# The first indirect gather of the routed experts placed ahead of a unit's values, and at most five loads of q, k, v asked for at a time

## The chip, the core and the metric

The kernel runs on one core of a Trainium2 chip. The core has a matrix engine (TensorE, in the profile PE for the matmuls and PEld for the loading of weights), a vector engine (VectorE, DVE), an activation engine (ScalarE, ACT), a general engine (GpSimd, POOL) and a queue that only issues transfers (SyncE, SP). Sixteen DMA engines move the data. The metric is the device time of one execution in microseconds, as the median of several runs. One execution is profiled, and its trace tells of every instruction when it started, how long it took and what it waited for.

## What is computed

An attention block without softmax is followed by a mixture of experts with an early exit. Cut to what matters:

```python
# q, k, v: (8, 8, 576, 64) float32; g_norm: (64,)
kv  = einsum('bhsd,bhse->bhde', k, v)          # one 64x64 state per batch and head
o   = einsum('bhsd,bhde->bhse', q, kv)
rms = sqrt(mean(o * o, axis=-1) + 1e-6)
x   = (o / rms * g_norm)                       # to (4608 tokens, 512)

out = x.copy()
xc  = x[x @ w_skip > 0]                        # the tokens that are computed
logits = xc @ w_gate                           # 8 experts
e_idx  = argmax(logits, axis=1)
gate_w = softmax(logits)[e_idx]
for e in range(8):                             # w1[e]: 512x1024, w2[e]: 1024x512
    h = relu(xc[e_idx == e] @ w1[e])
    y[e_idx == e] = gate_w * (h @ w2[e])
out[x @ w_skip > 0] = xc + y
```

The tokens of an expert are known only once the logits are: the kernel numbers them, writes x to the output in memory, and fetches the rows of each expert from there by an indirect gather.

## The kernel before

**The attention part** goes through 36 units, numbered n = 0 to 35 (`NU`, line 433). A unit is a pair of 128-token tiles for half of the heads. Two units (u = 0 and 1) make up a pair of tiles, two pairs a batch, and after each four batches two more units take the ninth row of each group of nine tokens. The loop of lines 1035 to 1075 writes out the order of all engines by hand: what is emitted earlier stands earlier in the queue of its engine, and each engine works through its queue in order. In step n stand, one after the other: `turn(n + 1)`, the transposes of q for the next unit; `root(n - 1)`, the square root on ACT; the jobs put down for "early"; `values(n)`, the eight matmuls of q with the state into a PSUM tile and the square of the result on ACT; the jobs for "mid"; `squares(n)`, the reduce of these squares on DVE (line 531); the jobs for "squared"; `norm(n - 1)`, on DVE the reciprocal (line 545) and the multiplication (line 554, tile `xl`) for the unit before; the jobs for "pe", the small additions of `finish`; and at the end the jobs for "dve" and "end". Up to step 29 `squares(n)` stands behind `norm(n - 1)`; from step 30 (`THIRD + 2`, with `THIRD` = 28) it stands ahead of it and of the "squared" jobs.

`scale` (line 641) runs what `weigh` has put aside, the multiplication by g_norm on POOL (line 628). Called from `norm` it lets the POOL instruction wait for the reciprocal of that norm, and it puts down the store of a finished pair of tiles for a later step.

**Buffers.** The PSUM tiles of `values` come from a pool of two (`o_ps`), but units 30 and 33 (`THIRDS`) use the tile of the states, `sum_ps`, which is free by then. A unit's PSUM tile is free again when its norm has read it.

**The states** of batch b are summed up by `state` (line 387), in portions over several steps ahead of the batch's units, and stored in `kvd`.

**Loads.** `load_part` (line 116) issues one load of 288 KB on the SP queue. A batch has four of each of q, k and v: 96 loads in all. The first 32 (k, v of batch 0, q of 0, k, v of 1, q of 1, k, v of 2) are issued ahead of the loop. The buffers hold three batches of k and v and two of q; later loads wait for the buffer that a batch before has used. The stores of x and the loads of the experts' weights go through the same queue, which issues in order.

**The routing.** Tokens are numbered in three groups, after units 12, 22 and 36 (`ends`). The stream `gating(1)`, of the second group, gives out four pieces of DVE work at the end of each step; it ends with `early()` (line 913), which fetches the first 192 tokens of the first expert (`FIRST`, 128 and 64) among the tokens of the first 22 tiles, so that their first layer can start before the attention part ends. `early` makes two small tables on DVE (`ohc1`, `bv1`, lines 916 and 921), and then gives `put` to "mid" of step 30:

- `scale(30)`, 22 matmuls on the PE (line 941) that place row numbers into PSUM, and `turn(32)`, which the loop leaves out later;
- in "squared" of step 30, `put_rows`: the sum of two pieces of a row number on DVE (line 949), two index operations on DVE and the first gather, 128 rows, on POOL (lines 930, 932, 934); a matmul that moves the row numbers of the other 64 tokens (line 953); again two index operations and the second gather, a row being fetched in two halves.

`first_in` (steps 33 and 34, "pe") transposes the gathered rows (line 865), `first_layer_1` multiplies them with the first expert's w1 (line 876). The load of its w2 is issued in step 32, behind the last matmul of `values(32)`. `hits` (line 759) makes on DVE, in two halves of eleven tiles each, a table that is used after the attention part; the halves stand in "mid" of steps 31 and 33.

**Behind the attention part** the last group is chosen on DVE (lines 682 to 702), ranked on the PE (lines 713 to 719), numbered, and the experts follow, ordered by their number of tokens, on the PE with matmuls of lines 1180 to 1279.

Of the kernel before, what the change touches and what calls it, by code (L numbers as in the profile page):

```python
# [8 lines left out]
FP32 = mybir.dt.float32  # L9
BF16 = mybir.dt.bfloat16  # L10
I32 = mybir.dt.int32
AX = mybir.AxisListType
# [5 lines left out]
def kernel(  # L18
# [92 lines left out]
    g_ps = ps_g.tile([P, 512], FP32)  # L111
    GB = 4 * KD + 8 * G

    kts, vts, qts = {}, {}, {}

    def load_part(t, src, b, j):

        js = slice(j, j + 1)
        nc.sync.dma_start(
            out=t[:, js, :, :].rearrange("p j c d -> p j (c d)"),  # L120
            in_=src[b].rearrange("(j a) (p c) d -> (a p) j (c d)", a=2, c=C)[:, js, :])

    def load(pool, tag, src, b):
        t = pool.tile([P, 4, C, D], FP32, tag=tag, name=tag)
# [321 lines left out]

    late = []
    todo = {}
    WAIT = mybir.DependencyInfo(mybir.DependencyClass.Sync, mybir.DependencyReason.SCHED_ONLY)

    def at(step, part, job):
        todo.setdefault((step, part), []).append(job)
# [188 lines left out]
    def scale(n, behind=None, keep=0, eng=None):  # L641

        while len(late) > keep:
            job, nq, store = late.pop(0)
            ins = job(eng or nc.gpsimd)
            if behind:
                tc.add_manual_dep(ins.ins, behind.ins.name, WAIT, reason="VectorE's port is free then")
            store = store() if store else None
            if store:
                at(max(min(n + 2, NU + 1), store_from.get(nq, 0)), "end", store)  # L650
# [262 lines left out]
    def early():  # L913

        ohc = gat_pool.tile([P, NE, 2], BF16, tag="ohc1", name="ohc1")
        nc.vector.tensor_tensor(out=ohc[:, :, :], in0=hi_k[:, 0:NE].unsqueeze(2).to_broadcast([P, NE, 2]),
                                in1=colid_i[:, 0:2].unsqueeze(1).to_broadcast([P, NE, 2]),
                                op=ALU.is_equal)
        yield
        bv = gat_pool.tile([P, NE, 2, 2], BF16, tag="bv1", name="bv1")  # L920
        nc.vector.tensor_tensor(out=bv[:, :, :, :], in0=ohc[:, :, :].unsqueeze(3).to_broadcast([P, NE, 2, 2]),
                                in1=row_k[:, 0:NE, :].unsqueeze(2).to_broadcast([P, NE, 2, 2]),
                                op=ALU.mult)
        ps = g_ps[:, GB:GB + 4]

        def gather(ps, m, off):
            n = P // m
            src = keep.tile([P, 1], I32, name=f"src{m}")
            row = gat_pool.tile([P, 1], FP32, tag="row1", name="row1")
            nc.vector.tensor_scalar(out=row[:, :], in0=ps, scalar1=float(n), op0=ALU.mult,  # L930
                                    scalar2=part_of[m][:, 0:1], op1=ALU.add)
            nc.vector.scalar_tensor_tensor(out=src[:, :], in0=row[:, :], scalar=float(N * n),
                                           in1=row[:, :], op0=ALU.is_lt, op1=ALU.mult)
            nc.gpsimd.indirect_dma_start(
                out=x_of(xg0, off, m), out_offset=None, in_=cut_rows(m, KNOWN)[:, :],
                in_offset=bass.IndirectOffsetOnAxis(ap=src[:, 0:1], axis=0))

        def put():
            scale(now[0])
            for t in range(NE):  # L940
                nc.tensor.matmul(out=ps, lhsT=oha_k[:, t, :],
                                 rhs=bv[:, t, :, :].rearrange("p c i -> p (c i)"), start=(t == 0),
                                 stop=(t == NE - 1), skip_group_check=True)
            turn(now[0] + 2)
            turned_ahead.append(now[0] + 2)

            def put_rows():
                rows = gat_pool.tile([P, 2], FP32, tag="rows1", name="rows1")
                nc.vector.tensor_reduce(out=rows[:, :], in_=ps.rearrange("p (c i) -> p c i", i=2),
                                        axis=AX.X, op=ALU.add)  # L950
                gather(rows[:, 0:1], P, 0)
                more = g_ps[:, GB + 4:GB + 5]
                nc.tensor.matmul(out=more, lhsT=again[0, 64][:, :], rhs=rows[:, 1:2], start=True,
                                 stop=True, skip_group_check=True)
                gather(more, 64, P)
            assert now[0] == THIRD + 2
            at(now[0], "squared", put_rows)
        yield
        yield
        yield "mid", put  # L960

    load_kv(1)
    load_q(1)
# [62 lines left out]
    for part in range(2):  # L1026
        at(NU - 3 + part, "pe", lambda part=part: first_in(part))
    at(NU - 1, "early", lambda: first_layer_1(range(1), slice(0, P)))
    for part in range(2):
        at(NU - 5 + 2 * part, "mid", lambda part=part: known_at.append(  # L1030
            hits(part * NE // 2, NE // 2, colid_i, gat_pool, NE, known_at)))
    at(NU - 1, "end", first_rest)

# [1 line left out]
    for n in range(NU + 2):  # L1035
# [6 lines left out]
        if n < NU:  # L1042
            values(n)
        jobs(n, "mid")
        if THIRD + 2 <= n < NU:
            squares(n)
        jobs(n, "squared")
        done = norm(n - 1) if 1 <= n <= NU else None
        if n < THIRD + 2:
            squares(n)  # L1050
        jobs(n, "pe")
        if done:
            done()
# [601 lines left out]
```

## Time and profile before

| what | value |
|---|---|
| median of 3 runs | 369.1 us (367.73, 369.1, 369.5) |
| the profiled execution | 368.61 us, of which 366.7 us from the first to the last instruction |
| granted clock of the PE | 0.997 |
| busy: PE, DVE, ACT, POOL | 349.8, 247.6, 147.0, 123.2 us |
| moved by the DMA engines | 81.70 MB, 32808 packets, mean 223 GB/s |
| loads of q, k, v | 96 of 288 KB |
| the first indirect gather issued on POOL | 101.17 us |

The span goes from the first to the last instruction; the rest of the execution's time lies around it. Busy time is the time in which an engine had an instruction at work; a wait of an engine is put down to what ended last before it went on. Instructions that only issue a transfer are not busy time, and the time to landing runs from the issue to the signal that all of the transfer has arrived.

### The profile page before, as it was taken

What the parts mean: (1) busy time and instruction counts of PE and PEld (TensorE: products, weight loads), DVE (VectorE), ACT (ScalarE), POOL (GpSimd) and SP (SyncE); (2) the same over time, 40 slices, a digit from 0 to 9 for tenths busy, and PEclk for the clock granted to TensorE, in tenths of its full rate; (3) what the DMA queues carried; (4) which work ended last, traced back from release to release, by engine and by line L of the source; (5) the groups of instructions that cost most, each with busy time, mean ns of one, the idle gap of its engine ahead of it and who ended that gap; (6) DMA issues with size and microseconds to landing.
All of it is one profiled execution on the core that took longest, in us unless ns stands there. A gap on an engine that the chain in (4) does not pass through costs nothing.

```text
span 366.7 us, 9560 instructions
## 1 busy us (share of the span) xinstructions
PE 349.8 (95%) x3754; PEld 304.6 (83%) x3754; DVE 247.6 (68%) x630; ACT 147.0 (40%) x424; POOL 123.2 (34%) x201
## 2 busy tenths in 40 slices
PE   8979998999899998999999999999999999999993
PEld 4768887889779667599879988989988998989982
DVE  2646678678889553875937676686776776878821
ACT  2537675677855323345104402511431430531410
POOL 8037677757784170223032102303203203002002
PEclk9999999999999999999999999999999999999998
DMA  7999999999969479782526437365563662601001
GB/s 258 378 389 389 391 384 389 394 351 305 348 214 362 121 255 374 285 261 77 220 85 231 145 142 240 126 231 155 193 230 102 231 247 73 221 1 57 3 2 53
DMA packets 32808, 81.70 MB, mean 223 GB/s; under 512 B 3242, under 2 KB 3250, under 8 KB 32756
## 3 DMA queue, kind: packets, MB, share of 16 engines
q1 hardware_dynamic: 29264, 70.53, 54.2%
q0 software_dynamic: 3472, 10.48, 8.8%
q8 instruction: 31, 0.51, 0.5%
q14 instruction: 21, 0.17, 0.1%
q10 hardware_dynamic: 20, 0.02, 0.0%
HBM read 66.80 MB, written 14.48 MB: 222 GB/s over the span
## 4 chain that ended last, share of the span: by engine, by line
PE 79%; issue 7%; DMA 4%; DVE 3%; POOL 2%; ACT 2%; SPq 0%; POOLq 0%; DVEq 0%; ACTq 0%
PE bank L1279 45%; PE bank L1211 9%; PE o_ps L507 6%; DMA v<-in_v_dram 4%; PE sum_ps L387 4%; PE bank L1199 4%; PE q_ps L469 3%; PE bank L1180 2%; DVE xl L554 1%; DVE rs L531 1%; PE o_ps L488 1%; PE q_ps L876 1%; PE g_ps L876 1%; POOL xb L628 1%; PE g_ps L417 1%
## 5 line engine op out<-in xcount | busy, mean ns | idle before, releaser
L1289 ACT COPY p<-bank 128x128 f32<-128x128 f32 (+6 forms) x70 | 20.8, 297 | 96.8 <-PE bank L1279 89.3
L1279 PE MATMUL bank<-xt,w 128*128 128x128 f32 (+5 forms) x336 | 55.4, 288 | 0.4 <-DVE bank L1283 0.4
L1410 POOL DMA_INDIRECT out_dram<-xg,rows x14 | 14.0, 997 | 116.5 <-DVE xg L1407 114.2
L1279 PEld LDWEIGHTS bank<-xt,w 128*128 128x128 f32 x336 | 47.0, 190 | 2.3 <-DVE bank L1283 1.8
L1283 DVE TENSOR_TENSOR bank<-bank,p 128x128 f32<-128x128 f32 (+6 forms) x70 | 23.6, 337 | 30.0 <-PE bank L1279 27.6
L628 POOL TENSOR_TENSOR xb<-xl,g_b 128x512 f32<-128x512 f32 x26 | 31.7, 1221 | 15.0 <-DVE rs L545 12.1
L1279 PE MATMUL bank<-xs,s 128*128 128x128 f32 (+5 forms) x224 | 36.7, 289 | 0.0
L507 PE MATMUL o_ps<-kvd,qT 128*128 128x146 f32 x240 | 35.4, 289 | 0.7 <-DVE xl L554 0.5
L507 PEld LDWEIGHTS o_ps<-kvd,qT 128*128 128x128 f32 x240 | 31.4, 189 | 1.9 <-DVE xl L554 1.3
L1279 PEld LDWEIGHTS bank<-xs,s 128*128 128x128 f32 x224 | 31.1, 190 | 1.0 <-issue 0.5
L1211 PE MATMUL bank<-w,ht 128*32 128x128 f32 (+2 forms) x424 | 29.9, 313 | 0.0
L387 PE MATMUL sum_ps<-v,k 64*64 64x64 f32 x1152 | 24.5, 223 | 4.7 <-issue 4.3
L531 DVE TENSOR_REDUCE rs<-sq 128x8 f32<-128x512 f32 x36 | 24.5, 681 | 5.2 <-ACT sq L523 5.0
L387 PEld LDWEIGHTS sum_ps<-v,k 64*64 64x64 f32 x1152 | 20.2, 134 | 9.2 <-issue 6.1
L554 DVE TENSOR_TENSOR xl<-o_ps,rs 128x584 f32<-128x584 f32 x32 | 24.5, 766 | 3.9
L1211 PEld LDWEIGHTS bank<-w,ht 128*32 128x32 f32 (+2 forms) x424 | 18.2, 119 | 10.6 <-issue 7.2
L1279 PE MATMUL bank<-t,ht 128*128 128x256 f32 x112 | 27.0, 384 | 0.0
L1279 PE MATMUL bank<-w,ht 128*128 128x256 f32 x112 | 26.5, 380 | 0.0
L1171 POOL DMA_INDIRECT xg<-out_dram,src x14 | 13.9, 992 | 35.2 <-DMA out_dram<-xg,rows 19.0
L1279 PE MATMUL bank<-t,hs 128*128 128x256 f32 x112 | 25.3, 379 | 0.0
L523 ACT ACTIVATE sq<-o_ps 128x512 f32<-128x512 f32 x34 | 20.2, 595 | 11.3 <-PE o_ps L507 10.5
L1279 PEld LDWEIGHTS bank<-t,ht 128*128 128x128 f32 x112 | 20.8, 190 | 3.9 <-issue 1.2
(217 smaller groups left out, 671.9 us busy)
## 6 DMA issues: line engine op xcount, KB each, us to landing
w<-in_moe_w_dram SPq DMA_DIRECT2D x16, 2048.0 KB, 10.1
k<-in_k_dram SPq DMA_DIRECT2D x32, 288.0 KB, 6.0
v<-in_v_dram SPq DMA_DIRECT2D x32, 288.0 KB, 6.2
q<-in_q_dram SPq DMA_DIRECT2D x32, 288.0 KB, 6.0
out_dram<-xb SPq DMA_DIRECT2D x25, 256.0 KB, 5.9
out_dram<-w SPq DMA_DIRECT2D x8, 256.0 KB, 5.5
out_dram<-xb POOLq DMA_DIRECT2D x3, 256.0 KB
xg<-out_dram,src POOLq DMA_INDIRECT x16
```

What stands on the lines that cost most here:

```text
L387: nc.tensor.matmul(out=sum_ps[w * 64:(w + 1) * 64, a, u, :], lhsT=kt[r, 2 * u + w, c, :], rhs=vt[r, 2 * u + w, c, :], start=(c == 0), stop ...
L507: mm = nc.tensor.matmul(out=ps[:, w, 0:2 * PK].rearrange("p (r k) -> p r k", r=2)[:, :, cols], lhsT=qT[:, w, a, :], rhs=kvds[b % KVD][:, w ...
L523: nc.scalar.activation(out=sq[:, :, :, :], in_=heads(ps, G, G + 2 * D), func=ACT.Square)
L531: nc.vector.tensor_reduce(out=rs[:, :, :], in_=sq[:, :, :, :].rearrange("p x y (a d) -> p x (y a) d", a=2), axis=AX.X, op=ALU.add)
L554: nc.vector.tensor_tensor(out=xl[:, :, :, :].rearrange("p x y (a k) -> p x (y a) k", a=2), in0=ps[:, :, 0:2 * PK].rearrange("p x (h k) -> ...
L628: late.append((lambda eng: eng.tensor_tensor(out=xb[:, :, 4 * u * D:(4 * u + 4) * D].rearrange("p r (w x) -> p r w x", w=2), in0=xl[:, :, ...
L1199: nc.tensor.matmul(out=hps[:, cols], lhsT=w_sb[r][0][:, dc, f * P:(f + 1) * P], rhs=xt[:, dc, cols], start=(dc == 0), stop=(dc == DC - 1))
L1211: nc.tensor.matmul(out=yps[q * m:(q + 1) * m, 0:n], lhsT=ht(f)[:, off:off + m], rhs=w_sb[r][1][:, f, q * n:(q + 1) * n], start=(f == 0), s ...
L1279: nc.tensor.matmul(out=out, lhsT=lhsT(i), rhs=rhs(i), start=start and i == 0, stop=i == k - 1, skip_group_check=True)
L1283: nc.vector.tensor_tensor(out=to, in0=x, in1=y, op=ALU.add)
L1289: nc.scalar.copy(out=t, in_=x)
L1410: ins = nc.gpsimd.indirect_dma_start(out=cut_rows(m)[:, :], out_offset=bass.IndirectOffsetOnAxis(ap=rows[:, col:col + 1], axis=0), in_=x, ...
```

## The change

Two things are changed. First, `put` goes from "mid" to "early" of step 30: the 22 placing matmuls, the sum of the row number, the two index operations and the first gather stand ahead of `values(30)`. A second job, `again_more`, stands in "mid" of step 30: `turn(32)` and the matmul for the other 64 tokens. The second gather alone is left in "squared". `put` no longer calls `scale(30)`, so that the weighing of unit 28 is issued by `norm(29)`, behind the first gather and behind that norm's reciprocal. `squares(n)` stands ahead of `norm(n - 1)` only from step 32 on, and in steps 30 and 31 the "squared" jobs stand behind norm and squares. The second half of `hits` goes from step 33 to step 34.

Second, each load of q, k, v from the thirteenth on waits, on SP, for the landing of the fifth load before it. Stores and weights are not counted and not held by this themselves.

```diff
--- before.py
+++ after.py
@@ -111,14 +111,19 @@
     g_ps = ps_g.tile([P, 512], FP32)
     GB = 4 * KD + 8 * G
 
-    kts, vts, qts = {}, {}, {}
+    kts, vts, qts, loads = {}, {}, {}, []
+    PACED, DEPTH = 12, 5
+    WAIT = mybir.DependencyInfo(mybir.DependencyClass.Sync, mybir.DependencyReason.SCHED_ONLY)
 
     def load_part(t, src, b, j):
 
         js = slice(j, j + 1)
-        nc.sync.dma_start(
+        ins = nc.sync.dma_start(
             out=t[:, js, :, :].rearrange("p j c d -> p j (c d)"),
             in_=src[b].rearrange("(j a) (p c) d -> (a p) j (c d)", a=2, c=C)[:, js, :])
+        if len(loads) >= PACED:
+            tc.add_manual_dep(ins.ins, loads[-DEPTH].ins.name, WAIT, reason="a short queue")
+        loads.append(ins)
 
     def load(pool, tag, src, b):
         t = pool.tile([P, 4, C, D], FP32, tag=tag, name=tag)
@@ -446,7 +451,6 @@
 
     late = []
     todo = {}
-    WAIT = mybir.DependencyInfo(mybir.DependencyClass.Sync, mybir.DependencyReason.SCHED_ONLY)
 
     def at(step, part, job):
         todo.setdefault((step, part), []).append(job)
@@ -935,29 +939,29 @@
                 out=x_of(xg0, off, m), out_offset=None, in_=cut_rows(m, KNOWN)[:, :],
                 in_offset=bass.IndirectOffsetOnAxis(ap=src[:, 0:1], axis=0))
 
+        rows = gat_pool.tile([P, 2], FP32, tag="rows1", name="rows1")
+
         def put():
-            scale(now[0])
             for t in range(NE):
                 nc.tensor.matmul(out=ps, lhsT=oha_k[:, t, :],
                                  rhs=bv[:, t, :, :].rearrange("p c i -> p (c i)"), start=(t == 0),
                                  stop=(t == NE - 1), skip_group_check=True)
+            nc.vector.tensor_reduce(out=rows[:, :], in_=ps.rearrange("p (c i) -> p c i", i=2),
+                                    axis=AX.X, op=ALU.add)
+            gather(rows[:, 0:1], P, 0)
+            assert now[0] == THIRD + 2
+            at(now[0], "mid", again_more)
+
+        def again_more():
             turn(now[0] + 2)
             turned_ahead.append(now[0] + 2)
-
-            def put_rows():
-                rows = gat_pool.tile([P, 2], FP32, tag="rows1", name="rows1")
-                nc.vector.tensor_reduce(out=rows[:, :], in_=ps.rearrange("p (c i) -> p c i", i=2),
-                                        axis=AX.X, op=ALU.add)
-                gather(rows[:, 0:1], P, 0)
-                more = g_ps[:, GB + 4:GB + 5]
-                nc.tensor.matmul(out=more, lhsT=again[0, 64][:, :], rhs=rows[:, 1:2], start=True,
-                                 stop=True, skip_group_check=True)
-                gather(more, 64, P)
-            assert now[0] == THIRD + 2
-            at(now[0], "squared", put_rows)
-        yield
-        yield
-        yield "mid", put
+            more = g_ps[:, GB + 4:GB + 5]
+            nc.tensor.matmul(out=more, lhsT=again[0, 64][:, :], rhs=rows[:, 1:2], start=True,
+                             stop=True, skip_group_check=True)
+            at(now[0], "squared", lambda: gather(more, 64, P))
+        yield
+        yield
+        yield "early", put
 
     load_kv(1)
     load_q(1)
@@ -1026,8 +1030,8 @@
     for part in range(2):
         at(NU - 3 + part, "pe", lambda part=part: first_in(part))
     at(NU - 1, "early", lambda: first_layer_1(range(1), slice(0, P)))
-    for part in range(2):
-        at(NU - 5 + 2 * part, "mid", lambda part=part: known_at.append(
+    for part, (step, where) in enumerate(((NU - 5, "mid"), (NU - 2, "mid"))):
+        at(step, where, lambda part=part: known_at.append(
             hits(part * NE // 2, NE // 2, colid_i, gat_pool, NE, known_at)))
     at(NU - 1, "end", first_rest)
 
@@ -1042,12 +1046,12 @@
         if n < NU:
             values(n)
         jobs(n, "mid")
-        if THIRD + 2 <= n < NU:
+        if THIRD + 4 <= n < NU:
+            squares(n)
+        done = norm(n - 1) if 1 <= n <= NU else None
+        if n < THIRD + 4:
             squares(n)
         jobs(n, "squared")
-        done = norm(n - 1) if 1 <= n <= NU else None
-        if n < THIRD + 2:
-            squares(n)
         jobs(n, "pe")
         if done:
             done()
```

## Prediction

> **What bounds the kernel now.** I read the page first (shares, then the chain that ended last), then the list of waits of the PE and of the SP queue, then the order of time of single engines around the edited place. The columns of the last kind are start us, duration us, engine, line, operation, how many; in brackets the idle time before and what ended it.
>
> ```profile
> PE 349.8 (95%) x3754; PEld 304.6 (83%) x3754; DVE 247.6 (68%) x630; ACT 147.0 (40%) x424; POOL 123.2 (34%) x201
> PE 79%; issue 7%; DMA 4%; DVE 3%; POOL 2%; ACT 2%; SPq 0%; POOLq 0%; DVEq 0%; ACTq 0%
> q8 instruction: 31, 0.51, 0.5%
> ```
>
> TensorE is the bound on the whole: 79% of the chain is its own work. What moves the end must therefore shorten or lengthen a stretch in which the PE stands still or waits. In the attention part (to about 109 us) the PE has few such stretches:
>
> ```profile
> PE sum_ps L387 <- DMA v<-in_v_dram: 0.3, 1, 0.3
> ...
> 24.47 0.62 PE L387 MATMUL sum_ps<-v,k 64*64 64x64 f32 x25 [2.43 <-issue]
> 63.38 0.57 PE L387 MATMUL sum_ps<-v,k 64*64 64x64 f32 x21 [0.99 <-issue]
> 69.87 0.56 PE L387 MATMUL sum_ps<-v,k 64*64 64x64 f32 x19 [0.84 <-issue]
> ```
>
> Three idle times of 2.43, 0.99 and 0.84 us end with nothing that the profile shows; loads are waited for by name for 0.3 us only (one at the edited place, 0.81, is quoted below). Now the loads themselves, from the SP queue's waits, its issues in order of time, and two stretches (busy us of PE, PEld, DVE, ACT, POOL, then clock, DMA share, GB/s):
>
> ```profile
> SPq L119 <- DMA k<-in_k_dram: 9.2, 22, 0.9
> k<-in_k_dram SPq DMA_DIRECT2D x32, 288.0 KB, 6.0
> DMA to landing us min/median/max: 3.5/6.0/7.7
> 64.90 0.33 SPq L119 DMA_DIRECT2D v<-in_v_dram  x1
> 65.65 0.33 SPq L119 DMA_DIRECT2D k<-in_k_dram  x1
> 45.63 1.08 SPq L119 DMA_DIRECT2D k<-in_k_dram  x1
> SPq L119 <- PE q_ps L469: 1.9, 2, 1.4
> 65.00:70.00 5.00, 4.16 (x107) 3.66 (x108) 4.18 (x9) 2.84 (x8) 3.72 (x7) 1.00 1.05 392
> 105.00:110.00 5.00, 4.44 (x89) 3.78 (x88) 4.60 (x10) 2.92 (x8) 4.60 (x9) 1.00 0.90 281
> ```
>
> The reader is to see three things. An issue follows the one before by 0.75 us (64.90 to 65.65), which for 288 KB is 393 GB/s, the 392 of the window 65 to 70 (last column; the one ahead is the DMA share, 1.05): the loads run at one fixed rate while they last. They take 6.0 us to land; 6.0 / 0.75 is eight, so eight are in flight already, and the 22 waits of SP for earlier k loads are that limit. And where a load waits for a buffer (45.63, held for 1.08; longest by name 1.4), the queue behind it stands too.
>
> **The change, part by part.** First the order around step 30. VectorE, with the ACT, POOL and PE rows that feed it:
>
> ```profile
> 96.98 0.25 DVE L921 TENSOR_TENSOR bv<-ohc,row_k 128x88 bf16<-128x88 bf16 x1
> 98.16 0.68 DVE L531 TENSOR_REDUCE rs<-sq 128x8 f32<-128x512 f32 x1
> 99.69 0.69 DVE L531 TENSOR_REDUCE rs<-sq 128x8 f32<-128x512 f32 x1 [0.85 <-ACT sq L523]
> 100.29 0.15 DVE L949 TENSOR_REDUCE rows<-g_ps 128x2 f32<-128x4 f32 x1
> 100.99 0.22 DVE L930 TENSOR_SCALAR row<-g_ps,q_f 128x1 f32<-128x1 f32 x1
> 101.62 0.77 DVE L554 TENSOR_TENSOR xl<-o_ps,rs 128x584 f32<-128x584 f32 x1
> 102.30 0.42 DVE L759 TENSOR_TENSOR ohc<-colid_i,hi_k 128x264 bf16<-128x264 int32 x1
> 102.88 0.69 DVE L531 TENSOR_REDUCE rs<-sq 128x8 f32<-128x512 f32 x1 [0.15 <-ACT sq L523]
> 103.78 0.77 DVE L554 TENSOR_TENSOR xl<-sum_ps,rs 128x584 f32<-128x584 f32 x1
> 104.57 0.69 DVE L531 TENSOR_REDUCE rs<-sq 128x8 f32<-128x512 f32 x1
> 106.18 1.09 DVE L759 TENSOR_TENSOR ohc<-colid_i,hi_k 128x264 bf16<-128x264 int32 x1
> 107.19 0.68 DVE L531 TENSOR_REDUCE rs<-sq 128x8 f32<-128x512 f32 x1
> 114.04 0.27 DVE L702 TENSOR_TENSOR ohb<-eorder,fi 128x112 bf16<-128x112 f32 x1
> ...
> 99.08 0.58 ACT L523 ACTIVATE sq<-sum_ps 128x512 f32<-128x512 f32 x1
> ...
> 97.50 1.16 PE L507 MATMUL sum_ps<-kvd,qT 128*128 128x146 f32 x8
> 98.49 0.69 PE L941 MATMUL g_ps<-bv,oha_k 128*128 128x4 bf16 x22
> 100.50 0.38 PE L953 MATMUL g_ps<-rows,again 128*128 128x1 f32 x2 [0.81 <-DVE rows L949]
> 105.70 0.60 PE L865 MATMUL q_ps<-ident,xg 128*128 128x128 f32 x4
> 108.93 0.74 PE L517 MATMUL o_ps<-kvd,q 64*64 64x73 f32 x32 [0.51 <-DVE xl L554]
> 114.50 0.38 PE L713 MATMUL g_ps<-top,ident 128*128 128x120 f32 x2
> ...
> 98.77 1.19 POOL L628 TENSOR_TENSOR xb<-xl,g_b 128x512 f32<-128x512 f32 x1
> 101.17 1.09 POOL L934 DMA_INDIRECT xg<-out_dram,src  x1 [1.21 <-DVE src L932]
> 102.56 1.01 POOL L934 DMA_INDIRECT xg<-out_dram,src  x1 [0.30 <-DVE xl L554]
> 105.79 1.18 POOL L628 TENSOR_TENSOR xb<-xl,g_b 128x512 f32<-128x512 f32 x1
> ```
>
> Step 30 begins on DVE at 98.84 (98.16 + 0.68, squares of unit 29). Before, DVE then idles 0.85 us, because the order has switched at this step from norm before squares to squares before norm, and the squares of unit 30 need ACT's square of the same step (99.08 + 0.58). Then squares 0.60 (99.69 to 100.29), row sum and two index operations 0.70 (to 100.99), the second gather's two 0.33 (to about 101.32), the norm of unit 29 0.98 (to 102.30), half the hits, squares of unit 31 from 102.88.
>
> After, no instruction is added or removed on DVE or PE; they change places. The 22 placing matmuls (0.69, and 0.6 start to start) go ahead of unit 30's values (97.50 to 98.49 before); their last operand is written at 97.23 (96.98 + 0.25). So the sum is there at about 98, and 0.8 us later, at 98.84, DVE reaches it, so that the sum is hidden by squares 29. DVE goes on without idle: 98.85 + 0.70 = 99.55 for the first index, against 100.99. The gather on POOL starts at about 99.8 instead of 101.17: **1.4 us earlier**. It no longer has the weighing at 98.77 (1.19) ahead of it; that one comes behind it, at about 100.9, held by the reciprocal of unit 29. Then norm 29 (0.98) to 100.5, squares of unit 30 (its values end 0.6 later on PE, 98.49 + 0.6 = 99.1, ACT's square 0.58 after that, so no wait) to 101.1, the second gather's two to 101.45, hits to 101.9, norm 30 (about 1.1: from 102.88 + 0.60 to 104.57 before) to 103.0, squares 31 to 103.6. Here the switch to squares first comes, at step 32 now, and with it the wait that was at step 30: root of unit 31 and square of unit 32 on ACT, 1.0 us from the end of one reduce to the start of the next (102.88 + 0.69 to 104.57 before). Squares 32 start at 104.6, where they start before: 104.57. **The 0.85 us idle is not removed but moved two steps on**; nothing is gained on DVE.
>
> The bounds of this: hits cost 0.42 at 102.30, when POOL was between its gathers, and 1.09 at 106.18, beside a weighing (105.79). After, the first half stands at 101.5 beside the weighing that was pushed behind the first gather. So the sum of this part is 0 with the low row and +0.5 to +0.7 with the high one; the mean of rows nearest to it, some +0.3 on DVE, is what I take. The SBUF page of the Trainium skill (SBUF — State Buffer, Who interferes with whom) says why: a VectorE operation with two SBUF inputs and a POOL operation that reads SBUF exclude one another for the whole instruction. By that rule the moved hits would pay the whole rest of the weighing, near the 1.09 row; the trace agrees at 106.18.
>
> The second half of the hits goes from step 33 to 34: about 1.0 us (106.18 to 107.19) leaves the place ahead of squares 33 and stands behind norm 32. DVE is packed there (4.60 of the 5 us from 105 to 110), so its end stays. What comes earlier is norm 32, and with it the buffer that the PE waits for 0.51 us at 108.93; the PE, busy with the first hidden columns until 108.42 (108.93 - 0.51), gains that 0.5. But the PE's next fixed point is L713 at 114.50, which needs the choice (114.04 + 0.27 = 114.31). Of the 0.5 only 0.2 can pass. With +0.3 of hits ahead of it the two about cancel: **-0.1 for the whole rearrangement, bounds -0.4 and +0.6.** The 0.81 us wait at 100.50 goes too, but it ends in the same DVE chain.
>
> Who uses the gather that is now earlier? L865, at 105.70, with no idle ahead of it; the gather was in time before. The PE reaches it maybe 1 us earlier and the gather 1.4 us earlier. On POOL, what is queued behind the first gather (weighing, second gather, the small adds) is done by about 103.1 instead of 103.6, so no store is later. The load of w2 follows unit 32's values, some 0.6 us earlier; the list of the PE's waits up to 145 us names no w: 0.
>
> Second, the pace. From the thirteenth load on, a load waits on SP for the fifth before it; behind it in that queue stand the stores and, at the end, the weight load of the first expert, which waits for the order of the experts and comes after the last q load: not touched. Five in flight at 0.75 us each are 3.7 us. As long as a load issued with four ahead lands within 3.7, the rate stays: the emptiest queue gave 3.5 (the minimum). So the loads lose nothing, each only lands 3.7 instead of 6.0 after an issue that comes 2.2 us later: **0**. The cover that goes is the depth: a stall of SP for a buffer could last 2.5 us (6.0 - 3.5) without the DMA running dry, now 0.2. Such stalls are 1.08 at 45.63 and 1.9 in two waits for q_ps; less 0.2 each that is some 2.4 us of DMA time at most; PE, on which they wait, is then the later one. I take 0, bounds -1.8 (below) and +2.2.
>
> Sum against the profiled execution: 368.61 - 0.1 = 368.5 us (366.7 span and 1.9 around it). That execution lies 0.5 under the median of the runs, 369.1, which spread from 367.73 to 369.5. With the gain side of the pace wider than the loss side I forecast **368.6**.
>
> **The rivals.** *A shorter queue lets other transfers through (faster).* The three unexplained idles of the PE lie in bursts of small state matmuls, and the page lists 31 instruction transfers on a queue of their own, 0.51 MB, 16 KB each; if these wait behind what the loads have in flight, five instead of eight would bring them sooner. For it: all three idles are in the stretch where DMA is full. Against: no row ties these idles to such a transfer. Price: the idle of 24.47 precedes a stretch in which loads set the pace and is given back; those of 63.38 and 69.87 vanish: 0.99 + 0.84 = 1.8. With the -0.1: 369.1 - 1.9 = 367.2, and 366.0 if a part of the 2.43 goes too. The Trainium skill (DMA: Bandwidth & Descriptors, Queues, rings and completion order) speaks against it: each DMA engine takes the queues in turn, packet by packet, so a longer ring of loads would not hold up another queue. By that rule this rival gives 0; nothing in this profile tells when such a transfer was asked for.
>
> *The short queue starves (slower).* If a load with four ahead takes 4.0 us, a load lands every 0.80 instead of 0.75 us. That decides from 3.7 up; between 3.5 (empty queue) and 6.0 (eight deep) no row shows it. Of the 96 loads (32 each of k, v, q) 12 are not paced and the last 8 wait for buffers anyway; 76 x 0.05 = 3.8 us; the 0.3 us of named waits shows the loads ahead of the PE, and I let the PE keep off nearly half: +2.2, 371.3.
>
> *The hits meet the weighing in full (no change, upper end).* Both halves at 1.09: +0.6 on DVE, choice at 114.9, PE waits at L713: 369.1 + 0.4 = 369.5.
>
> *The gather is not what was waited for:* the change does what it says to the gather and nobody notices. That is in the forecast.
>
> **How the numbers follow.** Forecast 0.51, hits in full 0.11, queue lets others through 0.25, starving 0.13. A measurement of this kernel tells about 0.5% (1.8 us) from no change, so below 367.2 is faster and above 370.9 slower. The first two are within. The rival with gain sits on the edge and reaches under it with the idles of the early part, and the forecast has a tail there: 0.26 faster. Starving is 0.12 above the edge. Range: 366.0 (rival one with part of the first idle) to 370.8 (half-way into the starving); outside are the worst of either.
>
> **What would show it.** Right: the first indirect gather on POOL near 99.8; no idle of DVE at step 30 and one of about 0.9 between the squares of units 31 and 32; squares 32 near 104.6; L713 on PE within 0.3 of 114.5; loads landing in about 3.7 to 4 us at issues still 0.75 apart. Wrong: the idles ahead of L387 at 63 and 70 shrunk or gone (rival one), or issues 0.80 or more apart, DMA rate under 370 GB/s in 65 to 70 and named waits of the PE for k, v or q (starving).

## The result and the profile after

The changed kernel takes **382.65 us** (median of six runs, 380.51 to 386.46) against 369.05 us for the kernel before beside it (six runs, 367.73 to 370.72): ratio **1.035, 95% interval 1.0316 to 1.0385**. It is slower by some 13 us. Here and below a median is over all executions, and a ratio leaves out those that took over 1.5% more than the fastest of the same kernel. The forecast of 368.6 us was wrong, and so was the range. The rival with a chance of 0.13, the short queue that starves, named the mechanism and put it far too low (371.3 us).

The profiled execution took 383.28 us, of which 381.4 us from the first to the last instruction (366.7 before). Its page: the busy times and the chain that ended last by engine, for which the page of before has PE 349.8 and a chain of PE 79%, DMA 4%.

```profile
PE 358.0 (94%) x3754; PEld 311.2 (82%) x3754; DVE 248.8 (65%) x630; ACT 147.8 (39%) x424; POOL 124.7 (33%) x201
...
PE 67%; DMA 23%; issue 5%; DVE 2%; SPq 1%; POOL 1%; POOLq 0%; DVEq 0%
```

The PE's share of the chain fell from 79% to 67% and DMA's rose from 4% to 23%. PE is also busy for 8.2 us longer (358.0 against 349.8) with the same 3754 matmuls; where that comes from is shown further down. Now the loads of q, k and v: the spread of their times to landing, the waits of the SP queue at their line, and the PE's waits up to 150 us.

```profile
DMA to landing us min/median/max: 3.1/4.9/6.6
...
SPq L121 <- DMA v<-in_v_dram: 14.8, 22, 2.0
SPq L121 <- DMA q<-in_q_dram: 14.4, 23, 1.8
SPq L121 <- DMA k<-in_k_dram: 13.5, 25, 1.8
...
PE q_ps L473 <- DMA q<-in_q_dram: 8.0, 8, 2.9
PE q_ps L869 <- DMA xg<-out_dram,src: 2.9, 2, 1.6
PE sum_ps L392 <- DMA v<-in_v_dram: 2.0, 3, 1.1
```

With four loads ahead of it a load lands in 4.9 us at the median, not in the 3.7 that five loads at 0.75 us need. SP now stands 42.7 us for earlier loads (14.8 + 14.4 + 13.5). Before, it stood 25.5 us: the 9.2 for k that the prediction shows, and these two:

```profile
SPq L119 <- DMA v<-in_v_dram: 8.9, 22, 0.7
SPq L119 <- DMA q<-in_q_dram: 7.4, 18, 0.7
```

The PE waits by name for q and v for 10 us, where it waited 0.3. The rate shows it too. One stretch of before, then two of after (busy us of PE, PEld, DVE, ACT, POOL; then clock, DMA share, GB/s):

```profile
30.00:50.00 20.00, 20.00 (x374) 17.83 (x364) 13.83 (x28) 14.37 (x40) 14.86 (x29) 1.00 1.05 389
```

```profile
30.00:50.00 20.00, 16.55 (x319) 14.74 (x317) 9.63 (x19) 10.28 (x27) 10.04 (x18) 0.91 0.98 315
120.00:140.00 20.00, 20.00 (x165) 16.70 (x163) 11.74 (x33) 7.29 (x30) 4.10 (x6) 0.79 0.57 200
```

389 GB/s became 315. The clock column is the second finding: 0.91 and, behind the attention part, 0.79, where it was 1.00 before. Next, issues of the same loads on SP (the 13th, the 48th and the 88th, the last v), before and after:

```profile
8.19 0.63 SPq L119 DMA_DIRECT2D k<-in_k_dram  x1
36.30 0.33 SPq L119 DMA_DIRECT2D v<-in_v_dram  x1
70.03 0.33 SPq L119 DMA_DIRECT2D v<-in_v_dram  x1
```

```profile
9.96 0.33 SPq L121 DMA_DIRECT2D k<-in_k_dram  x1
42.68 0.33 SPq L121 DMA_DIRECT2D v<-in_v_dram  x1
83.37 0.33 SPq L121 DMA_DIRECT2D v<-in_v_dram  x1
```

From the 48th to the 88th, 40 loads went out in 33.7 us before (0.84 each) and take 40.7 us after (1.02 each); from the 13th to the 48th it was 0.80 each and is 0.93. 1.02 x 5 is 5.1 us: a landing of 4.9 and 0.2 until SP goes on. The last v load is issued 13.3 us later.

The edited place in order of time, of after: DVE, POOL, PE and SP.

```profile
110.69 1.41 DVE L936 SCALAR_TENSOR_TENSOR src<-row 128x1 int32<-128x1 f32 x1
112.02 0.42 DVE L763 TENSOR_TENSOR ohc<-colid_i,hi_k 128x264 bf16<-128x264 int32 x1
113.34 0.68 DVE L535 TENSOR_REDUCE rs<-sq 128x8 f32<-128x512 f32 x1
114.87 0.69 DVE L535 TENSOR_REDUCE rs<-sq 128x8 f32<-128x512 f32 x1 [0.85 <-ACT sq L527]
...
109.78 1.09 POOL L938 DMA_INDIRECT xg<-out_dram,src  x1 [1.36 <-DVE rs L549]
110.88 1.19 POOL L632 TENSOR_TENSOR xb<-xl,g_b 128x512 f32<-128x512 f32 x1
112.37 1.00 POOL L938 DMA_INDIRECT xg<-out_dram,src  x1 [0.30 <-DVE src L936]
...
107.69 1.16 PE L511 MATMUL sum_ps<-kvd,qT 128*128 128x146 f32 x8
116.06 0.63 PE L869 MATMUL q_ps<-ident,xg 128*128 128x128 f32 x4 [1.32 <-DMA xg<-out_dram,src]
118.95 0.66 PE L869 MATMUL q_ps<-ident,xg 128*128 128x128 f32 x2 [1.59 <-DMA xg<-out_dram,src]
130.14 0.38 PE L717 MATMUL g_ps<-top,ident 128*128 128x120 f32 x2
...
106.04 0.42 SPq L346 DMA_DIRECT2D w<-in_moe_w_dram  x1
112.23 0.39 SPq L356 DMA_DIRECT2D w<-in_moe_w_dram  x1
```

```profile
93.92 0.42 SPq L341 DMA_DIRECT2D w<-in_moe_w_dram  x1
103.73 0.39 SPq L351 DMA_DIRECT2D w<-in_moe_w_dram  x1
```

Paired with the prediction's rows this gives the lag of the changed kernel. Unit 30's values start 10.2 us later (97.50, 107.69), of which the placing matmuls that now stand ahead of them make 0.6: **9.6 us had been lost by then, to waits for loads and to the clock behind such waits.** Most of it came in two steps: the lag grows by 4.7 us between 35 and 40 us of the kernel before, and by 4.1 between 82 and 88, each time with a wait for loads and then 3.4 us at half clock (39.6 to 43.0 and 94.2 to 97.6 in the changed kernel). The matmul of L717 (L713 before) starts 15.6 us later (114.50, 130.14); so another 5 to 6 us are lost right at the edited place, where the PE waits twice for gathered rows (1.32 and 1.59 us, 2.9 in all above). The span ends 14.7 us later. And the first weight load of the first expert (w1) is issued 12.1 us later (93.92, 106.04), just ahead of the gathers.

### The profile page after: what moved, and what is told of

The parts are those of the page before. It is cut to its first block, busy times and chain, and to the rows that moved or that the text cites. A ratio compares the mean times of both kernels' runs of the same rounds, so it can differ in the third digit from the quotient of the medians.

```text
span 381.4 us, 9561 instructions
## 1 busy us (share of the span) xinstructions
PE 358.0 (94%) x3754; PEld 311.2 (82%) x3754; DVE 248.8 (65%) x630; ACT 147.8 (39%) x424; POOL 124.7 (33%) x201
## 4 chain that ended last, share of the span: by engine, by line
PE 67%; DMA 23%; issue 5%; DVE 2%; SPq 1%; POOL 1%; POOLq 0%; DVEq 0%
PE bank L1283 43%; DMA q<-in_q_dram 10%; PE bank L1215 9%; DMA k<-in_k_dram 8%; DMA v<-in_v_dram 4%; PE bank L1203 4%; PE o_ps L511 2%; PE bank L1184 2%; DMA xg<-out_dram,src 2%; PE g_ps L880 2%; PE q_ps L473 1%; PE sum_ps L392 1%; PE q_ps L880 1%; SPq L121 1%; PE g_ps L783 1%
## 5 line engine op out<-in xcount | busy, mean ns | idle before, releaser
L511 PE MATMUL o_ps<-kvd,qT 128*128 128x146 f32 x240 | 36.3, 294 | 0.7 <-DVE xl L558 0.5
L511 PEld LDWEIGHTS o_ps<-kvd,qT 128*128 128x128 f32 x240 | 32.2, 193 | 1.8 <-DVE xl L558 1.3
L473 PE MATMUL q_ps<-ident,q 128*128 128x128 f32 x128 | 22.6, 294 | 8.0 <-DMA q<-in_q_dram 8.0
L392 PE MATMUL sum_ps<-v,k 64*64 64x64 f32 x1152 | 25.0, 228 | 2.2 <-DMA v<-in_v_dram 2.0
L1175 POOL DMA_INDIRECT xg<-out_dram,src x14 | 15.0, 1072 | 36.0 <-DMA out_dram<-xg,rows 19.6
L476 ACT COPY qT<-q_ps 128x512 f32<-128x512 f32 x32 | 18.8, 587 | 19.9 <-PE q_ps L473 19.5
L392 PEld LDWEIGHTS sum_ps<-v,k 64*64 64x64 f32 x1152 | 20.8, 139 | 6.7 <-issue 2.6
L527 ACT ACTIVATE sq<-o_ps 128x512 f32<-128x512 f32 x34 | 20.3, 596 | 13.3 <-PE o_ps L511 10.0
```

The source lines that it names most:

```text
L392: nc.tensor.matmul(out=sum_ps[w * 64:(w + 1) * 64, a, u, :], lhsT=kt[r, 2 * u + w, c, :], rhs=vt[r, 2 * u + w, c, :], start=(c == 0), stop ...
L473: nc.tensor.transpose(out=ps[:, w, :, hf, :], in_=qts[b][:, 2 * u + w, c:c + 2, :], identity=ident[:, :])
L476: nc.scalar.copy(out=qT[:, :, :, :].rearrange("p w a t -> p (w a t)"), in_=ps[:, :, :, :, :].rearrange("p w a h t -> p (w a h t)"))
L511: mm = nc.tensor.matmul(out=ps[:, w, 0:2 * PK].rearrange("p (r k) -> p r k", r=2)[:, :, cols], lhsT=qT[:, w, a, :], rhs=kvds[b % KVD][:, w ...
L527: nc.scalar.activation(out=sq[:, :, :, :], in_=heads(ps, G, G + 2 * D), func=ACT.Square)
```

## The experiments

Ratios are to the kernel before on the same chip, with the 95% interval.

**One part each.** *Order alone* leaves out the pace:

```diff
-    PACED, DEPTH = 12, 5
+    PACED, DEPTH = 96, 5
```

> The changed kernel without its pace: only the order around step 30 is changed. If starving is the cause (the loads land every 0.88 us instead of 0.75 because five in flight share a round trip of about 4.4 us), this one is at 369.1 +- 1 us: the 0.85 us idle of DVE only moves from step 30 to step 32, and the first gather is issued near 99.8 us with the PE not waiting for it. If the order has a share in the loss (the second index operation took 1.41 us instead of 0.16 beside a weighing, and the PE waits 2.9 us for the gathers), it is 2 to 4 us slower than before.

Measured: 367.54 us, 1.0005 (0.9972 to 1.0037). *Pace alone* is the kernel before with the added wait in `load_part` and nothing else:

```diff
+        if len(loads) >= PACED:
+            tc.add_manual_dep(ins.ins, loads[-DEPTH].ins.name, WAIT, reason="a short queue")
+        loads.append(ins)
```

> The kernel before with only the pace of five added. Starving: loads land every 0.88 us, the attention part ends 9 to 10 us later, and with the clock's halves the whole is 12 to 15 us slower. If the order has a share, it is less than 11 us slower.

Measured: 377.68 us, 1.0273 (1.0213 to 1.0332). The order by itself costs and brings nothing that can be measured; the pace by itself makes most of the loss. It is 10.4 us slower, which by the expectation (under 11) points at a share of the order; but order alone shows none. Together they lose 3.5%, somewhat more than the sum, and no run here tells why (the intervals of pace alone and of both overlap).

**The depth.** In the changed kernel `DEPTH` is 6, and 7:

> The changed kernel with six loads in flight instead of five. Starving with a round trip of 4.4 us: 4.4 / 6 is 0.73 us, under the 0.75 us that a load takes, so the rate is back at 380 GB/s or more, and what is left is what stalls of the queue for buffers cost: 369 to 373 us. If it is not the number in flight but the added waits themselves on SP that cost (88 waits at some 0.13 us), it is still 8 us or more slower than before.

> The changed kernel with seven loads in flight. Starving: as without the pace, 368 to 370.5 us, the loads 0.75 us apart. If the added waits themselves cost: 8 us or more slower than before, as with five.

Measured: 374.51 us, 1.0188 (1.0132 to 1.0244) with six; 370.24 us, 1.0026 (0.9989 to 1.0063) with seven. With six the expectation was missed on both counts: it took a fixed round trip of 4.4 us, which gave 380 GB/s and 373 us at most, but the landing grew to 5.1 us. One stretch of each:

```profile
30.00:50.00 20.00, 17.06 (x331) 14.86 (x332) 11.85 (x23) 11.77 (x31) 12.77 (x24) 1.00 1.03 369
```

```profile
30.00:50.00 20.00, 19.80 (x370) 17.41 (x371) 13.02 (x27) 14.15 (x39) 14.05 (x29) 1.00 1.05 390
```

| loads asked for at a time | landing, median us | GB/s, 30 to 50 us | ratio |
|---|---|---|---|
| 5 (after) | 4.9 | 315 | 1.035 |
| 6 | 5.1 | 369 | 1.019 |
| 7 | 5.5 | 390 | 1.003 |
| not held (order alone) | 6.0 | 393 | 1.0005 |

With seven, 84 loads carry the same added wait as with five, and nothing measurable is lost: it is not the waits as such, it is how much is asked for. Each load more in flight adds only some 0.2 to 0.5 us to the landing, so the rate rises with the depth, up to 393 GB/s at about eight.

**Which loads.** In the changed kernel only the loads from the 49th on are held, or only those up to the 48th:

```diff
-        if len(loads) >= PACED:
+        if PACED <= len(loads) < 48:
```

(the other one has `PACED` = 48).

> The changed kernel, but only loads 48 to 95 wait for the fifth load before them; loads 12 to 47 go out as in the kernel before. Theory A, the PE falls behind where it stands close behind the loads, which is early (its lag behind the kernel before is +5.4 us at 50 us and hardly grows up to 82): load 48 is issued near 37.8 us as before, load 88 some 9 us later than before (41.2 us for loads 48 to 88 in the changed kernel, 32.3 in the kernel before), but the PE stands further behind the loads by then and takes most of the 9 us without a wait: lag of the PE at 80 us below 1 us, named waits for q or v 3 us at most, 368 to 372 us. Rival B, each load that is paced costs the PE its 0.2 us wherever it stands: 40 paced loads of 76, half of the loss, lag at 88 us near +5, 375 to 377 us.

> The changed kernel, but only loads 12 to 47 wait for the fifth load before them; later ones go out freely. Theory A (the early loads set the pace of the PE): load 48 is issued near 45 us, the PE lags by 4 to 5.5 us at 50 us; what comes behind is free again at 0.80 us a load, so the lag stays or shrinks to some 3, and with what the later load of w2's place costs the time is 372 to 376 us. Rival B (cost by the number of paced loads, 36 of 76): 374 to 376 us, but with a lag near +2.5 at 50 us. The two kernels of this pair tell A from B together: by A this one is clearly the slower of the two.

(The expected issue times of loads 48 and 88 are off: some stores were counted among the loads. By the loads alone, number 48 goes out at 36.30 us before and 42.68 after, as quoted above.) Measured: late loads held 375.67 us, 1.0231 (1.0173 to 1.0289); early loads held 371.94 us, 1.0144 (1.0101 to 1.0188). Together 3.75%, about the 3.5% of all. By theory A the second should have been clearly the slower, and it is the faster one. By rival B the two should have been nearly equal, both at 374 to 377 us. So neither holds. With the late loads held (w1's issue, the first row of L869 on PE, and two stretches before and after it):

```profile
103.67 0.42 SPq L346 DMA_DIRECT2D w<-in_moe_w_dram  x1
113.01 0.94 PE L869 MATMUL q_ps<-ident,xg 128*128 128x128 f32 x4 [2.79 <-DMA xg<-out_dram,src]
109.70:113.20 3.50, 0.71 (x7) 0.53 (x6) 3.23 (x7) 0.90 (x2) 3.32 (x7) 1.00 1.00 350
113.20:120.00 6.80, 5.51 (x79) 4.62 (x77) 2.26 (x4) 1.96 (x5) 4.50 (x10) 0.50 1.03 381
106.71 1.12 POOL L938 DMA_INDIRECT xg<-out_dram,src  x1 [3.94 <-DVE src L936]
xg<-out_dram,src POOLq DMA_INDIRECT x1, 6.2
```

The last two rows are the first gather on POOL and its landing. Theory A was too low on the PE's waits for these loads, 4.3 us for q and v where it allowed 3, and on the lag: at 70 us the same matmuls still start at the same time as before, but at 80 us they lag by 2.9, where it allowed 1 (3.4 us of half clock from 75.6 are included). Unit 30's values start at 103.69, so 5.6 us have been lost by then (97.50 before, 0.6 for the placing matmuls). The rest of the 10.3 us by which L717 is late (124.84 against 114.50) is lost at the gathers, which theory A left out. The late loads end later, and what stands behind them on SP does too. First, the stores of x ahead of w1, from which the gathers read, go out from 97.51 to 101.9 instead of from 88.46 to 92.9. The first gather's index is ready at 104.22, but the gather starts only at 106.71; with order alone it started 0.3 us after its index. The profile names the index as what ended the wait, but the POOL queue passes its last semaphore at 105.8, about when stores of 5.5 to 5.7 us to landing are in. Second, w1 goes out at 103.67 instead of 93.92, and the gather takes 6.2 us to land (3.6 with only the early loads held, where w1 goes at 99.70). That it shares the DMA engines with w1's 2 MB is likely but not shown, since no run moves w1 alone and w2 goes out at 108.23 as well. The PE waits 2.79 us for the gather and then runs at half clock for 6.8 us.

With the early loads held (an idle of the PE, and the stretches before and after it):

```profile
70.27 0.72 PE L392 MATMUL sum_ps<-v,k 64*64 64x64 f32 x21 [2.30 <-issue]
67.00:70.50 3.50, 1.20 (x58) 1.04 (x60) 2.27 (x8) 1.75 (x6) 2.03 (x4) 1.00 1.05 387
70.50:73.90 3.40, 3.40 (x34) 3.20 (x27) 0.88 (x2) 0.79 (x2) 1.20 (x3) 0.51 1.05 391
```

The last v load goes out at 76.52, 6.5 us later than before (70.03), all of it lost by the 48th (42.68 here too), and w1 follows at 99.70. The PE lags 5.6 us at 50 us, near theory A's 4 to 5.5, and 7.3 from 70 us on. After an idle of 2.30 us the PE's clock is 0.51 for the next 3.4 us. So held early loads delay the PE at once; held late loads delay it about half by waits for them and the clock, and half at the gathers, through what stands behind them.

**The gathers and w2.** With order alone the PE waits 1.2 us for the second gather. In the new order that gather stands behind a weighing on POOL (110.88 above) while unit 32's values come early, so w2, again 2 MB, is asked for at about the time of the second gather, where before it followed it by 1.2 us (102.56 on POOL, 103.73 on SP). Three kernels test this. *Order alone, with w2 held until the second gather has landed:*

```diff
-    at(NU - 4, "pe", lambda: load_second(0, valued[-1]))
+    at(NU - 4, "pe", lambda: load_second(0, gathered[1]))
```

> The new order without the pace, and the load of the first expert's w2 waits for the landing of the second gather instead of the values of unit 32. If that load overtakes the second gather (in the run without the pace the gather was issued at 105.91 and landed at 111.95, after the w2 load's issue at 106.30; the PE waited 1.2 us), the PE no longer waits for a gather, no half clock follows near 110 us, and the time is 0.5 to 2 us under the order alone, 365.5 to 367 beside a before of 367.3. If the late gather has another cause (its index operation, the queue of POOL), the PE still waits over 1 us and the time is as with the order alone.

*The kernel before, with w2 one unit earlier* (`n == NU - 5` in place of `NU - 4`):

> The kernel before, no pace and old order, with the w2 load issued behind the values of unit 31 instead of 32, so some 1.5 us earlier, ahead of the second gather. Overtaking: the second gather lands 4 us or more later than before, the PE waits 1 to 4 us for it, half clock follows in most executions, and the time is 2 to 6 us longer. If overtaking is not what delays: the same as before within 1 us.

*The changed kernel, pace and all, with w2 held:*

> The changed kernel, pace of five and all, with the w2 load behind the landing of the second gather. If the 5 us by which the whole change exceeds the pace alone (382.65 against 377.7) are the second gather's wait and the half clock behind it, this one is at 376 to 379 us, with at most the first gather waited for. If they are the order on VectorE, it stays at 381 or more.

Landing of the second gather (last column, us) in order alone, with w2 held, and in the old order with w2 early, there with the PE's wait for it:

```profile
xg<-out_dram,src POOLq DMA_INDIRECT x1, 6.0
```

```profile
xg<-out_dram,src POOLq DMA_INDIRECT x1, 2.9
```

```profile
xg<-out_dram,src POOLq DMA_INDIRECT x1, 7.6
PE q_ps L865 <- DMA xg<-out_dram,src: 3.2, 1, 3.2
```

The mechanism is shown: a w2 load beside it more than doubles the gather's landing, 2.9 against 6.0 and 7.6 us, in the old order as in the new. Brought into the old order, it costs time, as expected: 372.41 us, 1.0151 (1.0085 to 1.0217), though no half clock follows the wait in that profile. But curing it brings nothing: 370.34 us, 1.0098 (1.0066 to 1.0129) with w2 held, against 367.54 for order alone, whose profile has no half clock near 110 us either; and 379.15 us, 1.0346 (1.0292 to 1.0399) for the changed kernel with w2 held, though in its profile the PE no longer waits for a gather and L717 lags no more than unit 30's values (10.0 and 11.0 us). Where w2 is held, the stores behind it on SP wait with it, and the PE waits later for other experts' rows (L1184, 1.4 us); whether that is what takes the gain away is not shown. So w2's place does not explain why the two parts together lose more than their sum; that stays open.

**The weighing.** Held w2 and, in `put`, the weighing called first as in the kernel before:

```diff
         def put():
+            scale(now[0])
```

> As the first of these, and the weighing of unit 28 stands on POOL ahead of the first gather again, not between the two. If the second index operation waits for the weighing (0.88, 1.41 and 1.95 us in three runs against 0.16), it takes 0.2 us here, the second gather is issued about 1 us earlier, and the time is another 0.3 to 1 us lower than the first of these. If the chain is bound elsewhere: the same as that one.

Measured: 369.76 us, 1.0085 (1.0048 to 1.0122). Its index operation ahead of the second gather, and L717:

```profile
101.39 0.16 DVE L936 SCALAR_TENSOR_TENSOR src<-row 128x1 int32<-128x1 f32 x1
113.68 0.48 PE L717 MATMUL g_ps<-top,ident 128*128 128x120 f32 x2
```

The index operation takes 0.16 us, where it took 1.41 beside the weighing (110.69 and 110.88 above). The other one, beside the weighing that is now first, takes 0.79: the cost moves. Measured from unit 30's values, the second gather is issued only 0.1 us earlier than in the kernel with w2 held alone, not 1 us, and the two ratios can't be told apart. In this execution L717 starts 0.8 us earlier than before (113.68, 114.50), yet the ratio is 0.85% above before's. Why is not settled.

**Number or bytes.** Each load fetches two parts, 576 KB; not held, and then with at most three in flight:

```diff
-        js = slice(j, j + 1)
+        js = slice(j, j + 2)
...
-    PACED, DEPTH = 12, 5
+    PACED, DEPTH = 6, 3
```

> The changed kernel with no load held (as in order alone), and each load of q, k, v fetches two of the four parts of a tile: 48 loads of 576 KB in place of 96 of 288 KB, the same rows and packets. It is the yardstick of the next kernel. Rate 385 to 395 GB/s from 30 to 70 us as with single loads; a portion of the state may start up to one single load (0.75 us) later: 367 to 370 us.

> Loads of 576 KB as in the kernel of pairs, and from the seventh on a load waits for the third before it: 1.73 MB asked for at a time, as much as six single loads, but three in number. Theory A, the bytes in flight set the rate: 355 to 365 GB/s from 30 to 70 us as with six single loads, +1.5 to +2.5% on the kernel of pairs. Rival B, the number of loads in flight sets it (a fixed time between one landing and the next issue, paid per load, or 16 engines that must all have finished a load): with three in number the rate is clearly below that of five single ones, under 320 GB/s, and +4% or more. Rival C, a fixed time per issue that larger loads spread over more bytes: rate above 370 GB/s, +1% at most.

Measured: 368.27 us, 1.0017 (0.998 to 1.0054), and 380.51 us, 1.0333 (1.0244 to 1.0421).

```profile
30.00:50.00 20.00, 19.33 (x380) 17.16 (x379) 13.38 (x27) 14.05 (x38) 14.10 (x27) 1.00 1.05 394
```

```profile
30.00:50.00 20.00, 15.38 (x270) 14.09 (x269) 7.88 (x16) 9.09 (x24) 8.40 (x16) 0.83 0.93 303
```

394 GB/s not held, so twice the bytes in flight bring nothing over eight single loads. With three it is 303, near the 315 of five single loads and far from the 369 of six. Theory A, as written, is out, and B's +4% was not reached. What fits both kernels was not among the theories: when a load may go out, four single loads or two pairs are still under way, 1152 KB in each. It is what is left when SP goes on that seems to set the rate; one pair of kernels supports that, no more.

## Why the prediction was wrong

**The step that failed** is this: "As long as a load issued with four ahead lands within 3.7, the rate stays: the emptiest queue gave 3.5 (the minimum)." The condition was right and the row was not. 3.5 is one load with little ahead of it. With four ahead it is 4.9 at the median, and one load goes out per 0.93 to 1.02 us. The rows that the prediction shows had two points, 3.5 for a nearly empty queue and 6.0 for eight; the point for five lies between them, and the text took the lower end as if it were that point. A straight line through both (one load at 3.5, eight at 6.0) would have given 3.5 + 4/7 x 2.5 = 4.9. And "between 3.5 (empty queue) and 6.0 (eight deep) no row shows it" was wrong: the trace of before has the point, in its first loads, issued while the queue filled.

```profile
4.95 0.33 SPq L119 DMA_DIRECT2D k<-in_k_dram  x1
DMA to landing us min/median/max: 5.1/5.1/5.1
```

This is the seventh load. The second was in at 4.90 (issued at 1.20, 3.7 to land), the third not before 6.16 (1.66 and 4.5), so four were ahead of it, and it took 5.1 us, not 3.7.

**The rival "starves"** took 0.05 us a load, 3.8 us in all, and let the PE keep off half. Measured are 0.13 (13th to 48th) and 0.17 (48th to 88th), 13.3 us at the last v load, of which 9.6 reach the PE. "The 0.3 us of named waits shows the loads ahead of the PE" says only that they are ahead, not by how much. Its signs all came: issues over 0.80 apart, a rate under 370 (282 from 65 to 70 us), named waits for q and v.

**"behind it in that queue stand the stores and [...] the weight load of the first expert [...]: not touched"** failed as well. w1 goes out 12.1 us later because it stands behind loads that end later, and so do the stores of x ahead of it (99.87 instead of 88.46). The first gather, which reads what they store, starts 0.8 us after its index (108.95, 109.78), where it was 0.3 with order alone, and w1 goes out just ahead of it. The load of w2 was put at "some 0.6 us earlier [...]: 0"; that step is the second one missed: the second gather lands in 6.0 us in order alone, and in 2.9 with w2 held. That "the gather was in time before" was true of the kernel before and did not last.

**The order of step 30** came out near what was worked out, though the time alone can't show it: order alone is at 1.0005 for a forecast of -0.1 us, and its interval, -1.0 to +1.4 us, holds the bounds of -0.4 and +0.6 too. Its profile says it better: unit 30's values start 4.3 us later than before (101.77) and L717 4.4 (118.89), so the edited place costs 0.1 us, with 1.2 us of waiting for the second gather in it that the prediction put at nothing. In the changed kernel the first gather starts at 109.78, which less the lag of 9.6 us is 100.2, where 99.8 was forecast. The idle of 0.85 us is gone from step 30 and stands between the squares of units 31 and 32, 0.85 again (113.34, 114.87). The moved hits were to pay for the weighing behind the first gather; they took their 0.42 (112.02), and the index operation just ahead of them paid instead, 1.41 for 0.16. That agrees with the rule quoted from the Trainium skill (SBUF — State Buffer, Who interferes with whom) in kind, on another instruction than the one named.

**The rival "lets other transfers through"** gained nothing that shows in the time. In the changed kernel's profile the unexplained idles ahead of L392 (L387 before) are gone, but waits for q and v of 10 us stand in their place; with pace alone some are left (1.17 us at 70.52).

**The half clock** was in no step. It is a good part of the loss: the profiled clock fell from 0.997 to 0.977, which is 0.020 x 381 = 7.6 us of the PE's work, and PE's busy time rose by 8.2 us. Runs of one kernel go the same way: the changed kernel took 380.51 and 381.34 us at a mean clock of 0.981, and 382.02 to 384.19 in three executions at 0.977. Even its fastest run, 380.51, is 11 us above before, and part of the half clock lies under waits for loads, so the two shares can't be parted from these runs.

## What to carry to other kernels

The time to landing of a load depends on how many are in flight, so a limit on them is judged by a row at that depth or by a line between two depths, never by the emptiest queue; here the first loads, issued while the queue filled, had that row. A queue that is slowed moves everything behind it: ask what the load at its end will then meet. And a wait of the PE can cost twice, once itself and once in the clock behind it.

## What the hardware did that was not expected

**Short waits can halve the clock.** The stretch from 67.0 to 70.5 us of the kernel with the early loads held has PE busy for 1.20 of 3.50 us, with an idle of 2.30 ahead of 70.27; the next 3.4 us run at a clock of 0.51. In the kernel with the late loads held it is 0.71 of 3.50 us, and 0.50 over the next 6.8. In the changed kernel one of these came behind the gathers:

```profile
114.60:118.00 3.40, 1.44 (x38) 1.01 (x36) 2.87 (x6) 2.30 (x6) 3.14 (x7) 1.00 0.98 357
118.00:128.20 10.20, 9.25 (x63) 8.91 (x64) 7.10 (x20) 4.40 (x18) 4.15 (x7) 0.50 0.92 348
```

1.44 of 3.40 us busy, in two waits of 1.32 and 1.59 us, and then 10.2 us at 0.50. The Trainium skill (TensorE: Matmul & The Clock Gate, Part 1: The HAM clock gate) says that the clock halves after an idle window of about 3.4 us, and that windows run free of the kernel. The lengths here agree (3.4, 6.8, 10.2 are one, two and three windows), and so does it that an idle of 2.43 us in the kernel before (24.47) had no such price in its profile. But the windows ahead were not idle: PE was busy in them for 20% to 42%. Where the clock changes in a trace gives the phase of its windows, in steps of 3.41 us. In the kernel before, the idle of 2.43 us is parted between two of them (20.0 to 23.4 and 23.4 to 26.8 us, PE busy for 2.04 and 2.37 us); in order alone an idle of 2.15 us at the same place lies in one (21.3 to 24.7, busy for 1.27), and the clock is 0.51 over the next 3.4 us. In all fourteen profiles, half clock followed each full-clock window in which the PE was busy for 42% or less, and none of 54% or more; between 48% and 53% it went both ways. As the traces model busy time, the limit is near a half.

**The second gather beside a load of 2 MB** that is issued within 1 us of it lands in 5.9 to 7.7 us (eight profiles, 6.4 in the changed kernel), in 5.1 where the load comes 1.2 us behind it (pace alone), and without it in 2.9. The Trainium skill (DMA: Bandwidth & Descriptors, Queues, rings and completion order) has the engines take the queues in turn, packet by packet, and the prediction leaned on that rule against its first rival. By that rule, and with packets of equal length, turns between two queues would about double the 2.9 us of the small transfer, an estimate: 6.0 agrees with that, 7.7 is more. A fair turn does not spare a gather that the PE is about to wait for.
